# A third chunk without transposes: loading x transposed and normalising it in place, in an MLP beside a long convolution

## The chip, the cores and the metric

The kernel runs on one core of one Trainium2 chip. The metric is the device time of one execution in microseconds (us); the runs shown are the median of three. The engines are TensorE (PE, with PEld for its weight loads), VectorE (DVE), ScalarE (ACT), GpSimd (POOL) and SyncE (SP). Each works through its own queue strictly in the order written there. An instruction that waits holds up all behind it on its engine.

## The reference

```python
xn = _layernorm(x)                       # x = A_q, (1, 2048, 448)
# A: gated long convolution
k_shift = sum of 4 shifted k * shift_k   # causal, per channel
kv = k_shift * v
y  = irfft(rfft(kv, 4096) * rfft(ssm_k, 4096))[:2048] + kv * ssm_D
# B: MLP with the Mish activation
h  = xn @ w1 + b1                        # 448 -> 1792
b  = (h * tanh(softplus(h))) @ w2        # 1792 -> 448
return x + xn * y + b
```

All inputs and outputs are float32.

## The kernel before

**MLP.** The 2048 positions are cut into 8 chunks of 256 (two halves of 128), the hidden features into 7 pairs of 128-wide blocks. That gives 56 pairs of (chunk, block pair), worked through in order. Each pair has two slots (half steps): in the even one the first layer's 20 matmuls (`g1_mm`, line 510), in the odd one the activation (`mish`, line 518) and the second layer's 12 matmuls (`g2_mm`, lines 542 to 544) of the pair two before. Float32 accuracy comes from splitting each operand into a high part (a cast on ACT: ach, XH) and a low part (a subtraction on DVE: acl, XL) and multiplying three times. A chunk's second layer accumulates in two PSUM tiles, one for each half; DVE evacuates them into qt (`g2_evac`, L549, two instructions), and since there are only these two tiles, the next chunk's second layer may start only when the evacuation has freed them.

**The chunk's normalised, transposed x.** The first layer needs xn with features on the partitions. Chunks below `NT` (0 to 3) get it by transposes: bn_stats, bn_aggr and eps (L404, L407, L410: ve) on DVE, a power and the normalisation (L413, L417, L421) on POOL, eight PE transposes through PSUM (L462), and the split from PSUM (L474 on ACT, L472 on DVE). Chunks from `NT` on load x already transposed (`xT_load`, L432). Their mean and 1/std are computed on the same two DVE lines and by the power on POOL (mv<-ve), stored to DRAM by a DMA that POOL issues (`nt_store`, L440: MR), and loaded back by SP as a row broadcast to 128 partitions (`nt_row`, L443), one half at a time into one buffer (con). DVE then subtracts and multiplies in place (`nt_norm`, two L449 for each half), and the result is split (`nt_split`: L456 on ACT, L457 on DVE).

**Convolution.** Its first stage transforms eight groups of kv, KV0 to KV7, at the slots 24, 29, 34, 39, 44, 50, 55 and 59. Per group: four taps of the short convolution on DVE (L187, L190, L192 multiply, L197 adds, L200 multiplies with v), then 16 small matmuls (`f1_mm`, L144) into the PSUM tiles pq and pr, which ACT copies in part (L150) and DVE folds in two instructions (L154), and the result leaves by DMA. One multiplication of each group (the third tap) is done on POOL (`taps_pool`, L180): a one-element memset on DVE (L179), written just before the fold of the group ahead, lets it start, and the L197 behind the fold takes its result.

**What sets the order.** A plan by slots: `at` puts a step ahead of a slot's own work, `after` behind it. The tables at the head hold each step's place relative to the slot b where a chunk begins: q the query load, x the transposed load, stats, flush (what is left of the statistics is written out), row, norm and split for the two halves. The statistics' small instructions are handed out one by one between the taps (`dv`, the list `drip`). For chunk `NT` itself b is one slot later (line 665), and line 664 gives the tighter table `NT_ENDS` to the chunks 4 and 7. Line 674 and the lines above it write the plan down; `mlp_slot` (L557) holds the steps of the transposed chunks.

Of the kernel before, what the change touches and what calls it, by code (L numbers as in the profile page):

```python
# [19 lines left out]
NCHUNK = S // CH  # L20
# [9 lines left out]
I2_AT = {100: ((6, 7, 0, 1), 92, (95, 97, 98, 99), (0, 2, 0, 1)),  # L30
         108: ((2, 3, 4, 5), 101, (104, 105, 106, 107), (0, 1, 0, 1))}
LATE = 2
NT = 4
NT_AT = {"q": -5, "x": -1, "stats": -2, "flush": 0, "row": (4, 8), "norm": (7, 10), "split": (8, 11)}
NT_ENDS = dict(NT_AT, row=(4, 5), norm=(4, 7), split=(6, 8))
WARM_N = (448, 448, 448)
FILL_N = (224, 112, 96)

# [2 lines left out]
def tile_kernel(ctx: ExitStack, tc, q, qT, k, v, sk, hT, sD, w10, w1, w2, c_fib, c_g, c_gi, c_i2, out):  # L41
# [20 lines left out]
    E = dp.tile([NJ * 4, 64, D], F32, name="E")  # L62
    MR = {c: dp.tile([2, CH], F32, name="MR") for c in range(NT, NCHUNK)}

# [8 lines left out]
    def rs(c):  # L73
        return rstd[:, 2 * c:2 * c + 2] if c < NT else mv[:, 2 * c:2 * c + 2, 1]

# [26 lines left out]
    def dv(n=1):  # L102
        for _ in range(n):
            if drip:
                drip.pop(0)()
# [4 lines left out]
    def at(slot, fn, *args):  # L110
        plan.setdefault(int(slot), []).append((fn, args))

    def after(slot, fn, *args):
        plan2.setdefault(int(slot), []).append((fn, args))
# [278 lines left out]
    def xn_tile():  # L393
        return mp.tile([128, 4, CH], F32, name="xn", bufs=1)

    def ln_parts(c):
        st = mp.tile([128, 2, 6], F32, name="bst", bufs=2)
        ve = mp.tile([128, 2], F32, name="ve", bufs=2)
        if c < NT:
            XN[c] = xn = xn_tile().rearrange("p a b -> p (a b)").rearrange("p (j d) -> p j d", j=2)  # L400
        eng = nc.gpsimd if 0 < c < NCHUNK - 1 else V

        def stats(jj):
            V.bn_stats(st[:, jj], Q[c][:, jj])  # L404

        def aggr(jj):
            V.bn_aggr(mv[:, 2 * c + jj], st[:, jj])  # L407

        def eps(a, b):
            V.tensor_scalar(ve[:, a:b], mv[:, 2 * c + a:2 * c + b, 1], EPS, None, op0=ALU.add)  # L410

        def power(a, b):
            nc.gpsimd.tensor_tensor(rs(c)[:, a:b], ve[:, a:b], mhalf[:, a:b], op=ALU.pow)  # L413

        def norm(jj):
            j = 2 * c + jj
            eng.tensor_scalar(xn[:, jj, :D], Q[c][:, jj], mv[:, j, 0:1], rs(c)[:, jj:jj + 1],  # L417
                              op0=ALU.subtract, op1=ALU.mult)

        def tail(a, b, copy=eng.tensor_copy):  # L420
            copy(xn[:, a:b, D:], xn[:, a:b, D - 64:D])  # L421

        return stats, aggr, eps, power, norm, tail, ve
# [52 lines left out]
    def ln_T(c, jj):  # L476
        if jj == 0:
            dv(len(drip))
            x_tiles(c)
        p = pg()  # L480
        transposes(c, jj, p)
        for lo in range(2):
            x_split(c, jj, p, lo)
# [73 lines left out]
    def mlp_slot(s):  # L557
# [3 lines left out]
        if half == 0:  # L561
            if i < n:
                c, p = pairs[i]
                if c + 1 < NT:
                    if p == 0:
# [8 lines left out]
        else:  # L574
            if i < n:
                c, p = pairs[i]
                if p == NP - 2 and c + 1 < NT:
                    ln_T(c + 1, 0)
# [82 lines left out]
        GB[46 + i] = n  # L661

    for c in range(NT, NCHUNK):
        at_ = NT_ENDS if c in (NT, NCHUNK - 1) else NT_AT
        b = 2 * NP * (c - 1) + (1 if c == NT else 0)
        at(b + at_["q"], ln_load, c)
        at(b + at_["x"], xT_load, c)
        at(b + at_["stats"], nt_stats, c)
        at(b + at_["flush"], lambda: dv(len(drip)))
        for jj in range(2):  # L670
            at(b + at_["row"][jj], nt_row, c, jj)
            after(b + at_["norm"][jj], nt_norm, c, jj)
            after(b + at_["split"][jj], nt_split, c, jj)
# [28 lines left out]
    stats, aggr, eps, power, norm, tail, ve = ln_parts(0)  # L702
# [120 lines left out]
```

## Time and profile before

| | us |
|---|---|
| median of 3 runs | 359.58 (359.16 to 359.68) |
| the profiled execution | 359.25, of which its span is 357.5 |
| PE busy in the span | 351.8 (98%) |
| DVE busy | 269.7 (75%) |
| ACT busy | 157.0 (44%) |
| POOL busy | 76.1 (21%) |
| granted TensorE clock | 0.998 |

A row of a timeline gives the start (us from the span's start), the duration, engine, line, operation, out<-in, shape and count; in brackets stands the idle time ahead of it and what ended that. Matmuls overlap: the distance between their starts tells what they cost, not their duration. A row with count 2 is two instructions merged.

### The profile page before, as it was taken

The page shows a single profiled execution, that of the slowest core. Times are in us where ns is not written, and L with a number is a line of the kernel's source. Part 1 is how long each engine was busy: PE and PEld are TensorE (multiplying, and loading weights), DVE is VectorE, ACT ScalarE, POOL GpSimd, SP SyncE. Part 2 cuts the span into 40 slices and gives each one's busy share as a digit, 9 for nine tenths or more (in the row PEclk, how much of TensorE's full clock was granted, in tenths as well). Part 3 has the DMA queues.
Part 4 walks back from the last instruction along what each step waited for, and adds up shares of the span by engine and source line. Part 5 has one row for each costly group of instructions (what it writes and reads, how often), then busy time and mean ns, then how long its engine had stood idle before and what let it go on. Part 6 is the DMA issues. An engine that isn't in the chain of part 4 may idle for free.

```text
span 357.5 us, 7447 instructions
## 1 busy us (share of the span) xinstructions
PE 351.8 (98%) x3100; PEld 290.2 (81%) x3100; DVE 269.7 (75%) x371; ACT 157.0 (44%) x267; POOL 76.1 (21%) x81
## 2 busy tenths in 40 slices
PE   8999999999999999999999999999999999999995
PEld 2988888888888989888997758667775699979795
DVE  5989658999998899999537757756863933788942
ACT  4976552344232443343233453455445343354480
POOL 2037002821128240204000030011031116040030
PEclk9999999999999999999999999999999999999999
DMA  7998978749585536665969669999985386989076
GB/s 237 349 383 308 403 290 240 224 153 267 148 276 187 161 107 175 216 162 92 233 198 345 239 166 302 228 287 306 285 261 131 81 242 263 405 311 285 26 115 142
DMA packets 30227, 82.48 MB, mean 231 GB/s; under 512 B 3057, under 2 KB 15474, under 8 KB 30194
## 3 DMA queue, kind: packets, MB, share of 16 engines
q1 hardware_dynamic: 21410, 47.03, 38.7%
q0 software_dynamic: 4896, 22.95, 22.9%
q10 hardware_dynamic: 3888, 12.03, 12.6%
q8 instruction: 24, 0.39, 0.5%
q14 instruction: 9, 0.07, 0.1%
HBM read 53.55 MB, written 28.45 MB: 229 GB/s over the span
## 4 chain that ended last, share of the span: by engine, by line
PE 52%; DVE 5%; issue 1%
PE pq L510 7%; PE pg L542 7%; PE pg L544 7%; PE pg L543 6%; PE pp L510 5%; PE pr L510 4%; PE pp L233 3%; PE pr L233 3%; PE pp L272 2%; PE pg L510 2%; PE pq L233 2%; PE pr L272 1%; DVE x L197 1%; PE pp L326 1%; DVE acl L83 0%
## 5 line engine op out<-in xcount | busy, mean ns | idle before, releaser
L542 PE MATMUL pg<-w2h,ach 128*128 128x448 f32 x224 | 82.4, 368 | 0.0
L544 PE MATMUL pg<-w2h,acl 128*128 128x448 f32 x224 | 81.4, 363 | 0.0
L543 PE MATMUL pg<-w2l,ach 128*128 128x448 f32 x224 | 81.2, 363 | 0.0
L83 DVE TENSOR_TENSOR acl<-a,ach 128x512 fp32r<-128x512 f32 x56 | 38.8, 693 | 32.1 <-ACT ach L82 31.9
L518 ACT ACTIVATE a<-pg,b1t 128x256 f32<-128x256 f32 x66 | 27.9, 473 | 64.7 <-PE pg L510 57.9
L510 PE MATMUL pg<-XH,w1h 128*128 128x256 f32 x264 | 52.8, 283 | 0.1
L542 PEld LDWEIGHTS pg<-w2h,ach 128*128 128x128 f32 x224 | 41.9, 187 | 10.8 <-issue 6.5
L510 PEld LDWEIGHTS pg<-XH,w1h 128*128 128x128 f32 x264 | 41.3, 188 | 7.2 <-issue 5.6
L543 PEld LDWEIGHTS pg<-w2l,ach 128*128 128x128 f32 x224 | 42.1, 188 | 2.5
L544 PEld LDWEIGHTS pg<-w2h,acl 128*128 128x128 f32 x224 | 42.1, 188 | 2.4
L510 PE MATMUL pg<-XL,w1h 128*128 128x256 f32 x264 | 42.8, 277 | 0.0
L154 DVE TENSOR_TENSOR st<-pq,st 128x896 f32<-128x896 f32 x32 | 34.8, 1088 | 5.1 <-ACT st L150 4.5
L510 PEld LDWEIGHTS pg<-XL,w1h 128*128 128x128 f32 x264 | 35.9, 188 | 0.0
L82 ACT CAST ach<-a 128x512 fp32r<-128x512 f32 x56 | 34.8, 622 | 1.7
L180 POOL TENSOR_TENSOR x<-kr,skb 128x896 f32<-128x896 f32 x8 | 17.0, 2126 | 83.1 <-DVE x L179 70.5
L510 PE MATMUL pg<-XH,w1l 128*128 128x256 f32 x198 | 33.5, 278 | 0.0
L510 PEld LDWEIGHTS pg<-XH,w1l 128*128 128x128 f32 x198 | 27.6, 188 | 0.0
L197 DVE TENSOR_TENSOR x<-x 128x896 f32<-128x896 f32 x24 | 26.4, 1098 | 0.9 <-POOL x L180 0.3
L518 ACT ACTIVATE a<-pq,b1t 128x256 f32<-128x256 f32 x20 | 8.4, 472 | 31.8 <-PE pq L510 31.8
L283 POOL DMA_DIRECT2D E<-qe x14 | 8.7, 628 | 63.1 <-ACT qe L280 63.1
L150 ACT COPY st<-pr 128x896 f32<-128x896 f32 x16 | 14.5, 907 | 14.1 <-PE pr L144 12.1
L144 PE MATMUL pq<-x,con 32*64 32x448 f32 x128 | 15.9, 560 | 0.5 <-DVE x L200 0.5
(138 smaller groups left out, 601.3 us busy)
## 6 DMA issues: line engine op xcount, KB each, us to landing
Dkv<-st ACTq DMA_DIRECT2D x16, 448.0 KB, 6.3
ah<-Dh SPq DMA_DIRECT2D x8, 896.0 KB, 8.4
av<-Dkv SPq DMA_DIRECT2D x8, 896.0 KB, 8.8
e<-E POOLq DMA_DIRECT2D x8, 896.0 KB, 7.3
E<-qe POOLq DMA_DIRECT2D x14, 448.0 KB, 6.0
kr<-in_k_dram SPq DMA_DIRECT2D x10, 448.0 KB, 6.6
Dh<-st ACTq DMA_DIRECT2D x10, 448.0 KB, 6.4
x<-in_hT_dram SPq DMA_DIRECT2D x8, 448.0 KB, 6.6
```

Source lines behind the costliest of these rows:

```text
L82: nc.scalar.copy(h, raw)
L83: V.tensor_sub(l, raw, h)
L144: nc.tensor.matmul(ps[h][64 * jj:64 * jj + 64, b, :D], f1[rg:rg + 32], x[rg:rg + 32, jj], start=True, stop=True, tile_position=(rg, 64 * jj))
L154: f(st[:, n], e, st[:, 1])
L180: nc.gpsimd.tensor_mul(o, KR[g - u // 2], skb[:, u:u + 1].to_broadcast([128, 2, D]))
L197: V.tensor_add(KV[g], KV[g], o)
L233: nc.tensor.matmul(p[32 * t:32 * t + 32, r, :D], g[rs, t, c], a[rs, t], start=True, stop=True, tile_position=(64 * r, 32 * t))
L510: nc.tensor.matmul(ps[n], l, r, start=all(m[0] != n for m in seq[:n_]), stop=all(m[0] != n for m in seq[n_ + 1:]))
L518: nc.scalar.activation(a[:, n], ps[n], AF.Mish, bias=b1t[:, 2 * p + n:2 * p + n + 1])
L542: nc.tensor.matmul(ps, ah[:, n, cs], w2h[:, f], start=f == 0, stop=False)
L543: nc.tensor.matmul(ps, ah[:, n, cs], w2l[:, f], start=False, stop=False)
L544: nc.tensor.matmul(ps, al[:, n, cs], w2h[:, f], start=False, stop=f == NF - 1)
```

## The change

Chunk 3 joins the chunks that are loaded transposed (`NT` is 3). Its slot b is 29, and chunk 4's, which was 43, is now 42, since only the first such chunk gets the extra slot. The tight table now goes to the chunks 3, 4 and 7 under the name `NT_SOON`; its numbers are unchanged. Chunk 5 gets a table of its own: the query load three slots sooner, statistics and flush two slots sooner.

```diff
-NT = 4
+NT = 3
 NT_AT = {"q": -5, "x": -1, "stats": -2, "flush": 0, "row": (4, 8), "norm": (7, 10), "split": (8, 11)}
-NT_ENDS = dict(NT_AT, row=(4, 5), norm=(4, 7), split=(6, 8))
+NT_SOON = dict(NT_AT, row=(4, 5), norm=(4, 7), split=(6, 8))
+NT_HOW = {c: NT_SOON for c in (3, 4, 7)}
+NT_HOW[5] = dict(NT_AT, q=-8, stats=-4, flush=-2)
...
     for c in range(NT, NCHUNK):
-        at_ = NT_ENDS if c in (NT, NCHUNK - 1) else NT_AT
+        at_ = NT_HOW.get(c, NT_AT)
         b = 2 * NP * (c - 1) + (1 if c == NT else 0)
```

What that does to the queues is seen in the order of the instructions. Line numbers of the changed kernel are higher by 2. First POOL's whole stretch between chunk 2's normalisation and the convolution's second part, before:

```order
L180 TENSOR_TENSOR x<-kr,skb 128x896 x3
L413 TENSOR_TENSOR rstd<-ve,mhalf 128x2
L417 TENSOR_SCALAR xn<-qt,mv,rstd 128x448
L421 COPY xn<-xn 128x64
L417 TENSOR_SCALAR xn<-qt,mv,rstd 128x448
L421 COPY xn<-xn 128x64
L180 TENSOR_TENSOR x<-kr,skb 128x896
L413 TENSOR_TENSOR mv<-ve,mhalf 128x2
L440 DMA MR<-mv 128x2x2
L180 TENSOR_TENSOR x<-kr,skb 128x896 x3
L413 TENSOR_TENSOR mv<-ve,mhalf 128x2
L440 DMA MR<-mv 128x2x2
```

The same stretch of POOL after the change:

```order
L182 TENSOR_TENSOR x<-kr,skb 128x896
L415 TENSOR_TENSOR mv<-ve,mhalf 128x2
L442 DMA MR<-mv 128x2x2
L182 TENSOR_TENSOR x<-kr,skb 128x896 x3
L415 TENSOR_TENSOR mv<-ve,mhalf 128x2
L442 DMA MR<-mv 128x2x2
L182 TENSOR_TENSOR x<-kr,skb 128x896 x2
L415 TENSOR_TENSOR mv<-ve,mhalf 128x2
L442 DMA MR<-mv 128x2x2
L182 TENSOR_TENSOR x<-kr,skb 128x896
```

Chunk 3's power moved from behind KV3's tap (the third of the first row) to ahead of KV2's, now with a store instead of two normalisations; chunk 5's power moved ahead of KV7's tap, which was the last of three. On DVE, from the acl ahead of KV2's taps to the L197 behind the next fold (KV1's), before:

```order
L83 TENSOR_TENSOR acl<-a,ach 128x512
L187 TENSOR_TENSOR x<-kr,skb 128x896
L190 TENSOR_TENSOR x<-kr,skb 128x448
L192 TENSOR_TENSOR x<-kr,skb 128x448
L197 TENSOR_TENSOR x<-x 128x896
L83 TENSOR_TENSOR acl<-a,ach 128x512
L179 MEMSET x 1x1
L154 TENSOR_TENSOR st<-pq,st 128x896 x2
L197 TENSOR_TENSOR x<-x 128x896
```

The same stretch of DVE after the change:

```order
L406 BN_STATS bst<-qt 128x6
L189 TENSOR_TENSOR x<-kr,skb 128x896
L406 BN_STATS bst<-qt 128x6
L192 TENSOR_TENSOR x<-kr,skb 128x448
L409 BN_AGGR mv<-bst 128x2
L194 TENSOR_TENSOR x<-kr,skb 128x448
L409 BN_AGGR mv<-bst 128x2
L199 TENSOR_TENSOR x<-x 128x896
L412 TENSOR_SCALAR ve<-mv 128x2
L85 TENSOR_TENSOR acl<-a,ach 128x512
L181 MEMSET x 1x1
L156 TENSOR_TENSOR st<-pq,st 128x896 x2
```

Chunk 3's five statistics moved in between KV2's taps, ahead of the memset; they stood in the fold of KV2 and behind it. On PE two rows of four transposes, ahead of and behind the second layer's matmuls of slot 39, are gone, and nothing else moves. The rest of DVE's and SP's order follows the tables: four L449 and two L457 of chunk 3 among the taps of KV3 and KV4, and chunk 3's transposed load and two row loads on SP.

## The prediction

> **What bounds the kernel now.** I read the page's first two parts (PE busy in every slice, clock full), then the busy time by stretches, then the timelines of TensorE (PE), VectorE (DVE) and GpSimd (POOL).
>
> ```profile
> 94.00:126.00 32.00, 32.00 (x253) 28.37 (x252) 30.00 (x43) 11.31 (x21) 12.24 (x7) 1.00 0.70 209
> ```
>
> The columns are the stretch, its length, then the busy time of PE, PEld, DVE, ACT and POOL. Around the edit PE never rests and DVE works 30.00 of 32 us. PE sets the end; DVE hardly keeps up with it as long as the key-value groups (KV0 to KV7) run. Wherever DVE falls behind, PE waits. It does once:
>
> ```profile
> 156.80 0.62 PE L510 MATMUL pg<-XL,w1h 128*128 128x256 f32 x4
> 157.34 0.59 PE L144 MATMUL pq<-x,con 32*64 32x448 f32 x2
> 167.86 0.62 PE L510 MATMUL pg<-XL,w1h 128*128 128x256 f32 x4
> 169.01 0.59 PE L144 MATMUL pq<-x,con 32*64 32x448 f32 x2 [0.53 <-DVE x L200]
> 161.27 0.06 DVE L179 MEMSET x<- 1x1 f32 x1
> 162.26 1.38 DVE L410 TENSOR_SCALAR ve<-mv 128x2 f32<-128x2 f32 x1
> 164.55 1.08 DVE L197 TENSOR_TENSOR x<-x 128x896 f32<-128x896 f32 x1
> 167.86 1.09 DVE L200 TENSOR_TENSOR x<-x 128x896 f32<-128x896 f32 x1
> 161.49 2.12 POOL L180 TENSOR_TENSOR x<-kr,skb 128x896 f32<-128x896 f32 x1 [12.62 <-issue]
> ```
>
> From the last matmuls of a pair to the next group's first one PE takes 157.34 - 156.80 = 0.54; at KV7 it takes 1.15, since L200 ends at 168.95. The stall is 0.61. Its root stands above: chunk 5's two-column ve ran 1.38 and ended at 163.64, just when POOL's tap ended (163.61).
>
> **Transposes gone: -0.76.** The only work that leaves PE is chunk 3's eight transposes. The stretch that holds them is set against the same stretch of slots 55 and 56, without transposes:
>
> ```profile
> 113.26 0.62 PE L510 MATMUL pg<-XL,w1h 128*128 128x256 f32 x4
> 120.14 0.62 PE L510 MATMUL pg<-XL,w1h 128*128 128x256 f32 x4
> 162.92 0.63 PE L510 MATMUL pg<-XL,w1h 128*128 128x256 f32 x4
> ```
>
> 120.14 - 113.26 = 6.88 against 162.92 - 156.80 = 6.12: 0.76, all on the path. POOL's two normalisations go too; POOL is not on the path.
>
> **Chunk 3's statistics, from slot 34 to 27.** The order shows two bn_stats, two bn_aggr and ve spread over KV2's taps; on POOL the power and the MR store now stand ahead of KV2's tap.
>
> ```profile
> L404 DVE BATCH_NORM_STATS2 bst<-qt 128x6 f32<-128x448 f32 x16 | 9.6, 618 | 2.7 <-DMA qt<-in_q_dram 2.7
> L407 DVE BATCH_NORM_AGGREGATE mv<-bst 128x2 f32<-128x6 f32 x16 | 2.6, 173 | 0.1
> L410 DVE TENSOR_SCALAR ve<-mv x9: 153/169/1376, 4.5 to 260.5; 128x2 f32<-128x2 f32 x7, 128x1 f32<-128x1 f32 x2
> 87.47 0.68 DVE L83 TENSOR_TENSOR acl<-a,ach 128x512 fp32r<-128x512 f32 x1
> 90.48 1.09 DVE L197 TENSOR_TENSOR x<-x 128x896 f32<-128x896 f32 x1
> 95.41 1.15 DVE L549 TENSOR_TENSOR qt<-pg,qt 128x448 f32<-128x448 f32 x2
> 96.47 2.21 DVE L154 TENSOR_TENSOR st<-pq,st 128x896 f32<-128x896 f32 x2
> 128.41 0.69 DVE L83 TENSOR_TENSOR acl<-a,ach 128x512 fp32r<-128x512 f32 x1
> 128.57 1.09 POOL L413 TENSOR_TENSOR mv<-ve,mhalf 128x2 f32<-128x2 f32 x1 [8.21 <-DVE ve L410]
> 129.96 0.83 POOL L440 DMA_DIRECT2D MR<-mv  x1 [0.30 <-POOL mv L413]
> 131.39 2.12 POOL L180 TENSOR_TENSOR x<-kr,skb 128x896 f32<-128x896 f32 x1 [0.60 <-DVE x L179]
> 163.72 0.72 POOL L413 TENSOR_TENSOR mv<-ve,mhalf 128x2 f32<-128x2 f32 x1
> L413 POOL TENSOR_TENSOR rstd<-ve,mhalf x5: 552/730/1555, 4.7 to 107.4; 128x2 f32<-128x2 f32 x3, 128x1 f32<-128x1 f32 x2
> 97.84 0.36 PE L542 MATMUL pg<-w2h,ach 128*128 128x448 f32 x1
> 100.34 0.59 PE L144 MATMUL pq<-x,con 32*64 32x448 f32 x2
> ```
>
> DVE's share: 2 x 0.62 + 2 x 0.17 + 0.17 = 1.75, less 0.08 each, since the next instruction starts that much before an end (the two L549 take 1.15 and L154 starts 1.06 after them): 1.35. So ve, now just ahead of the acl at 87.47, ends at about 88.90. Behind it on POOL come the power, a gap of 0.30, the store's 0.83 and only then the tap's 2.12. The power has two prices in these rows, 1.09 and 0.72, and took 1.55 at the most (the last L413 row, at 107.4). In the row with 1.09 an acl was running, and in the new order an acl follows ve at once, so I take 1.09, with 0.72 and 1.55 as ends. The tap then ends at 88.95 + 1.09 + 0.30 + 0.83 + 2.12, about 93.32, and L197, which adds it, runs at 93.36, not 90.48: DVE is 2.88 late, of which the wait for POOL is 1.53.
>
> The Trainium skill, page "SBUF — State Buffer", section "Who interferes with whom", says that a DVE instruction with two SBUF inputs keeps out a GpSimd instruction that reads SBUF until it ends, whichever issued first holding the port. By that rule the power would end some 0.56 behind the acl, and the two rows agree (0.72 beside a fold that reads PSUM); without it the median of 0.73 would do, and the sum below would be 0.36 lower.
>
> Who waits: chunk 2's first second-layer matmul (97.84) needs the accumulator that the first L549 frees. That ends at 95.41 + 0.62 + 2.88 = 98.91, PE starts 0.06 later: a stall of 1.13. KV2's matmuls (100.34) need the fold that ended at 98.68, now 101.56: 0.14 more than the 1.13. PE is 1.27 late, and 0.51 once the transposes are gone.
>
> **Normalisation and split of chunk 3, chunk 4's steps a slot sooner.**
>
> ```profile
> 109.57 1.49 DVE L200 TENSOR_TENSOR x<-x 128x896 f32<-128x896 f32 x1
> 113.82 1.33 DVE L197 TENSOR_TENSOR x<-x 128x896 f32<-128x896 f32 x1
> 116.06 0.69 DVE L472 TENSOR_TENSOR XL<-pg,XH 128x512 fp32r<-128x512 f32 x1 [0.92 <-ACT XH L474]
> 117.45 0.69 DVE L83 TENSOR_TENSOR acl<-a,ach 128x512 fp32r<-128x512 f32 x1 [0.70 <-ACT ach L82]
> 124.32 1.09 DVE L200 TENSOR_TENSOR x<-x 128x896 f32<-128x896 f32 x1
> 134.99 1.14 DVE L549 TENSOR_TENSOR qt<-pg,qt 128x448 f32<-128x448 f32 x2
> 139.97 1.41 DVE L449 TENSOR_TENSOR xn<-xn,con 128x512 f32<-128x512 f32 x2
> 143.10 0.69 DVE L83 TENSOR_TENSOR acl<-a,ach 128x512 fp32r<-128x512 f32 x1 [0.72 <-ACT ach L82]
> 128.00 0.59 PE L144 MATMUL pq<-x,con 32*64 32x448 f32 x2
> 136.47 0.36 PE L542 MATMUL pg<-w2h,ach 128*128 128x448 f32 x1
> ```
>
> Until KV4's L200, DVE gains two pairs of L449 (2 x 1.33 start to start) and part of chunk 4's statistics (two bn_stats, one bn_aggr: 1.17). It loses chunk 3's statistics at their old place (1.35), its idle gaps at the transposes (0.92 + 0.70) and what two instructions took above 1.09 while POOL normalised (0.40 + 0.24). The low halves L457 and L472 cost the same. Lateness: 2.88 + 2.66 + 1.17 - 1.35 - 1.62 - 0.64 = 3.10. L200 ends at 125.41 + 3.10 = 128.51, and PE wants it at 128.00 + 0.51 = 128.51: no stall, but no margin.
>
> Chunk 2's evacuation is next. Chunk 4's statistics no longer lie in between: lateness 3.10 - 1.17 = 1.93. Its first L549 ends at 137.53; PE, due at 136.98, starts at 137.59: 0.61. PE's lateness is 1.12.
>
> What moves on SP's queue is the transposed load, the two row loads and the query load of chunk 3, and the steps of chunks 4 and 5. The second row load waits for the first half's normalisation, since both halves use one row buffer, and behind it stand the key load of KV4 and chunk 4's query load; at chunk 4 the first row comes ahead of KV6's key load, and the second ahead of chunk 2's result, chunk 5's query load (which reuses the result's buffer and waits for it to leave) and KV6's value load. I price all of it at nothing: DVE, 2 to 3 us late, comes to each load's first use later than before, and a key that is late by less than that keeps nobody. Without this cover it is the second rival. On ACT the two casts XH<-xn take the place of two casts from PSUM; ACT has room (11.31 of 32 us).
>
> **Chunk 5's statistics, two half steps sooner.** ve now precedes the memset that starts the tap, so it should take 0.17. The tap then bounds the fold: L197 runs at 161.27 + 0.15 + 2.12 + 0.04 = 163.58 relative to the old times, 0.97 sooner than 164.55. With the gap of 0.72 absorbed DVE is 1.93 - 0.72 - 0.97 = 0.24 late at KV7: L200 ends at 169.19. PE, without the old stall, wants it at 168.40 + 1.12 = 169.52. The stall of 0.61 is gone. If ve still met a tap, 0.97 would come back, less the margin of 0.33.
>
> **Sum.** -0.76 + 1.13 + 0.14 + 0.61 - 0.61 = +0.51. The profiled execution took 359.25 (span 357.5 and 1.75 around it), 0.33 below the median of 359.58. So 359.76 in its terms and 360.1 on the median. With the power at 0.72 or 1.55 it is +0.14 or +0.97: 359.7 to 360.6.
>
> **Rivals.** The first: the tap isn't held up, because POOL runs it beside the store or DVE has more room than I found. For it: no row shows a tap directly behind a store. Against: POOL's rows never overlap, and its order is fixed. Then DVE is only 1.35 late: L549 ends at 97.38, before 97.84, and the fold at 100.03, before 100.34. PE is 0.76 early; KV4 holds (126.98 against 127.24); chunk 2's evacuation is 0.39 late and PE loses some 0.35. With the old stall gone that is -0.76 + 0.35 - 0.61 = -1.02: 358.6, faster.
>
> The second: the row of chunk 4 comes late.
>
> ```profile
> DMA to landing us min/median/max: 3.2/5.2/8.6
> DMA to landing us min/median/max: 3.6/4.7/9.2
> ```
>
> The first row is the MR store's, the second the row load's. Chunk 4's store leaves at about 130.6 and DVE reaches the first L449 at 139.97 - 0.60 + 1.93 = 141.30 (the acl that stood before it now follows). The medians make 140.5, in time. If the two together take over 10.7, DVE waits, and the key load behind the row on SP's queue comes late as well; at 8.6 + 4.7 it is 2.6, of which 0.33 is covered: +0.51 + 2.27, 362.4, slower. For it: in chunk 5 the store took the 8.6. Against: at chunk 4's place it has landed near the minimum before. The Trainium skill, page "DMA: Bandwidth & Descriptors", section "Anatomy of one DMA — SWDGE (gpsimd) path", gives 2.0 us and a size term for a GpSimd DMA; this 2 KB store would by that estimate land in 2.0, and the rival could not occur. The rows say 3.2 at least, so they decide, and it stays open.
>
> **How the numbers follow.** The forecast gets 0.55, the first rival 0.25, the second 0.20. Within 0.2% is 358.86 to 360.30, about what a measurement of this kernel can tell from no change. Of the forecast's 0.55 some 0.12 lies above (power beyond 1.3, or KV4 without margin). Faster 0.25, same 0.43, slower 0.32. The range runs from just under the first rival, 358.3, to 361.6, inside the second; the forecast's own is 359.7 to 360.6.
>
> **What would show it.** On POOL the power, the store and a tap in a row near 89 to 93, and L197 waiting 1.5 for POOL; PE waiting for L549 at 98 and at 137; no wait for L200 at KV7 and ve at 0.17; the stretch around 113 to 120 shorter by 0.76. I am wrong if L197 doesn't wait, if PE waits for L200 at KV4, or if L449 waits for its row.

## The result and the profile after

| | us |
|---|---|
| before, median of 11 runs | 359.41 (359.05 to 359.89) |
| after, median of 11 runs | 360.19 (359.95 to 360.86) |
| ratio after to before | 1.0021, 95% interval 1.0011 to 1.0031 |
| span of the profiled execution, before and after | 357.5 and 358.8 |

The change makes the kernel 0.78 us slower. That is 0.21%, with an interval from 0.11 to 0.31%, so it is slower than before, and just about at the 0.2% that the prediction took as the least it could tell from no change. The forecast was 360.1, with 358.3 to 361.6 as its range. Of all the executions behind this document one was disturbed, 899.18 us of the kernel with three more transfers, and its ratio is taken without it.

The first fence shows timeline rows of the changed kernel around KV2's taps: DVE, then POOL, then PE. Its line numbers are higher by 2 (L199 is the old L197, L551 the old L549, L412 ve, L415 the power, L442 the MR store, L182 POOL's tap).

```profile
89.08 0.16 DVE L412 TENSOR_SCALAR ve<-mv 128x2 f32<-128x2 f32 x1
89.15 0.69 DVE L85 TENSOR_TENSOR acl<-a,ach 128x512 fp32r<-128x512 f32 x1
93.73 1.09 DVE L199 TENSOR_TENSOR x<-x 128x896 f32<-128x896 f32 x1 [1.76 <-POOL x L182]
98.67 1.15 DVE L551 TENSOR_TENSOR qt<-pg,qt 128x448 f32<-128x448 f32 x2
89.32 1.08 POOL L415 TENSOR_TENSOR mv<-ve,mhalf 128x2 f32<-128x2 f32 x1 [13.45 <-DVE ve L412]
90.70 0.83 POOL L442 DMA_DIRECT2D MR<-mv  x1 [0.29 <-POOL mv L415]
91.56 2.14 POOL L182 TENSOR_TENSOR x<-kr,skb 128x896 f32<-128x896 f32 x1
97.95 0.62 PE L512 MATMUL pg<-XL,w1h 128*128 128x256 f32 x4
99.34 0.47 PE L544 MATMUL pg<-w2h,ach 128*128 128x448 f32 x1 [0.77 <-DVE qt L551]
99.65 0.36 PE L545 MATMUL pg<-w2l,ach 128*128 128x448 f32 x1
101.99 0.59 PE L146 MATMUL pq<-x,con 32*64 32x448 f32 x2
```

Power, store and tap stand in a row on POOL. The tap ends at 93.70, which is 4.46 behind ve; the working had 4.42. L199 waits 1.76 for it. PE then waits for L551: from the last first-layer matmuls to the second layer it takes 99.34 - 97.95 = 1.39, and where nothing is late 0.45 (97.60 - 97.15 in the fence of the first experiment), so the stall is 0.94. From there to KV2's matmuls it takes 2.65 against 2.50 before: 0.15 more. Of that, 0.11 lies in the first step behind the stall, which takes 0.31 (99.34 to 99.65) where before it took 0.20 (97.84 to 98.04).

The next rows of the changed kernel belong to the missing transposes, KV4, chunk 2's evacuation and KV7.

```profile
114.91 0.62 PE L512 MATMUL pg<-XL,w1h 128*128 128x256 f32 x4
121.03 0.63 PE L512 MATMUL pg<-XL,w1h 128*128 128x256 f32 x4
127.86 1.09 DVE L202 TENSOR_TENSOR x<-x 128x896 f32<-128x896 f32 x1
129.01 0.59 PE L146 MATMUL pq<-x,con 32*64 32x448 f32 x2
137.02 0.62 PE L512 MATMUL pg<-XL,w1h 128*128 128x256 f32 x4
137.94 0.44 PE L544 MATMUL pg<-w2h,ach 128*128 128x448 f32 x1 [0.31 <-DVE qt L551]
160.18 0.17 DVE L412 TENSOR_SCALAR ve<-mv 128x2 f32<-128x2 f32 x1
169.42 0.62 PE L512 MATMUL pg<-XL,w1h 128*128 128x256 f32 x4
169.96 0.59 PE L146 MATMUL pq<-x,con 32*64 32x448 f32 x2
```

The stretch that held the transposes takes 6.12 in place of 6.88: 0.76 gained. At KV4 the matmuls start at 129.01, 0.06 behind the end of L202 (128.95); from PE's last matmul before them it takes 0.38 (128.63 to 129.01) in place of 0.30 (127.70 to 128.00), so PE waits 0.08 there. Chunk 2's L551 costs 0.92 - 0.45 = 0.47. Chunk 5's ve takes 0.17, and KV7's matmuls follow after 0.54: the old stall of 0.61 is gone.

So far the terms, without KV4's, make -0.76 + 0.94 + 0.15 + 0.47 - 0.61 = +0.19. Most of the rest is at the end of the program. The fence has, of the changed kernel and then of the kernel before, the last evacuations on DVE and the group of SP's semaphore waits once the last result has landed (the columns of the group: times of one in ns, first and last start).

```profile
353.72 0.62 DVE L551 TENSOR_TENSOR qt<-pg,qt 128x448 f32<-128x448 f32 x1 [3.51 <-PE pg L546]
L820 SPq EVENT_SEMAPHORE  x8: 28/28/28, 357.5 to 357.9; - x8
352.67 0.62 DVE L549 TENSOR_TENSOR qt<-pg,qt 128x448 f32<-128x448 f32 x1 [3.51 <-PE pg L544]
L818 SPq EVENT_SEMAPHORE  x3: 28/28/28, 356.5 to 356.6; - x3
```

From the first of the last two evacuations to the end it is 358.8 - 353.7 = 5.1 after and 357.5 - 352.7 = 4.8 before. SP works off eight waits instead of three, 0.06 apart: 5 x 0.06 = 0.30. No term of the forecast had that. With it the sum is +0.5. About 0.25 more lies in three steps of 0.08: KV4's wait, the first second-layer matmul behind chunk 2's stall, which takes 0.28 to the next (137.94 to 138.22) instead of 0.20, and a slightly slower first layer near 174. Together these make about 0.75, near the 0.78 measured. One further difference of the two profiled executions isn't the change's: PE comes 0.56 later to KV0's matmuls near 48, ahead of everything that was edited. In the other profiles that same place lies between 0.3 earlier and 1.2 us later than in the profile of before.

### The profile page after: what moved, and what is told of

Same layout as the page of the kernel before. It is cut to its first block, busy times and chain, and to the rows that moved or that the text cites. A ratio compares the mean times of both kernels' runs of the same rounds, so it can differ in the third digit from the quotient of the medians.

```text
span 358.8 us, 7434 instructions
## 1 busy us (share of the span) xinstructions
PE 352.3 (98%) x3092; PEld 289.8 (81%) x3092; DVE 270.2 (75%) x375; ACT 156.6 (44%) x267; POOL 73.5 (20%) x78
## 4 chain that ended last, share of the span: by engine, by line
PE 60%; issue 4%; DVE 3%; POOL 1%
PE pg L544 8%; PE pg L546 8%; PE pg L545 8%; PE pq L512 7%; PE pg L512 6%; PE pp L512 5%; PE pr L512 4%; PE pr L235 3%; PE pp L235 3%; PE pp L274 2%; PE pq L235 2%; PE pr L274 1%; PE pp L328 1%; DVE x L199 1%; PE pq L146 1%
## 5 line engine op out<-in xcount | busy, mean ns | idle before, releaser
L182 POOL TENSOR_TENSOR x<-kr,skb 128x896 f32<-128x896 f32 x8 | 17.0, 2130 | 68.1 <-DVE x L181 42.1
L199 DVE TENSOR_TENSOR x<-x 128x896 f32<-128x896 f32 x24 | 26.2, 1090 | 3.0 <-POOL x L182 2.3
L415 POOL TENSOR_TENSOR mv<-ve,mhalf 128x2 f32<-128x2 f32 x5 | 5.4, 1084 | 73.1 <-DVE ve L412 73.1
```

The lines of the kernel that those rows point to most:

```text
L182: nc.gpsimd.tensor_mul(o, KR[g - u // 2], skb[:, u:u + 1].to_broadcast([128, 2, D]))
L199: V.tensor_add(KV[g], KV[g], o)
```

## The experiments

**The tap first.** The working held the order on POOL responsible. This kernel changes only that.

```diff
+        held = [lambda: (power(0, 2), nt_store(c))]
+        if c == 3:
+            HELD.extend(held)
         drip.extend([lambda: stats(0), lambda: stats(1), lambda: aggr(0), lambda: aggr(1),
-                     lambda: (eps(0, 2), power(0, 2), nt_store(c))])
+                     lambda: (eps(0, 2), *[f() for f in held if c != 3])])
...
             after(t, taps_pool, g + 1, 2)
+        if g == 1:
+            after(t, lambda: HELD.pop()())
```

> The changed kernel with one thing in another order: on POOL chunk 3's power and MR store stand behind KV2's tap, not ahead of it; DVE, PE, ACT and SP keep their order. My theory (the tap is held up by power and store): L199 behind KV1's fold no longer waits 1.76 for POOL, DVE is 1.76 sooner, chunk 1's L551 and the fold come in time, and chunk 2's L551 too, so the three stalls of 0.94, 0.15 and 0.47 go: 360.2 - 1.56 = 358.6, faster than before by 0.2%. Rival (DVE's longer list alone makes it late; POOL's order is no matter): 360.2 as the change. Second rival (chunk 3's row is now late, since the store leaves some 2.3 later; in the changed kernel it landed 5.0 ahead of its use): the three stalls go, but L451 waits for its row; it has about 1.0 to spare, and each us above that comes back at a later stall.

Measured: 358.68, against 359.27 before on the same chip, ratio 0.9976 (0.9968 to 0.9985). Rows of POOL, DVE and PE:

```profile
89.18 2.13 POOL L182 TENSOR_TENSOR x<-kr,skb 128x896 f32<-128x896 f32 x1 [14.12 <-PE pg L549]
91.25 0.72 POOL L415 TENSOR_TENSOR mv<-ve,mhalf 128x2 f32<-128x2 f32 x1
92.27 0.83 POOL L445 DMA_DIRECT2D MR<-mv  x1 [0.29 <-POOL mv L415]
91.34 1.09 DVE L199 TENSOR_TENSOR x<-x 128x896 f32<-128x896 f32 x1 [0.18 <-POOL x L182]
97.15 0.62 PE L515 MATMUL pg<-XL,w1h 128*128 128x256 f32 x4
97.60 0.36 PE L547 MATMUL pg<-w2h,ach 128*128 128x448 f32 x1
```

With the same work in the same order on DVE, L199 waits 0.18 instead of 1.76, and PE goes on after 0.45. At chunk 2's L551 PE takes 0.52 (135.05 to 135.57), so of the stall of 0.47 only 0.07 is left. The two ratios, 1.0021 and 0.9976, lie 0.0045 or 1.6 us apart, as the three stalls (0.94 + 0.15 + 0.47 = 1.56) would have it. The change is slower because of the order of three POOL instructions. DVE's longer list alone doesn't make it so, and no wait for chunk 3's row took the place of the stalls.

**Chunk 3's statistics one half step sooner still.** The same end by the table, one line added.

```diff
+NT_HOW[3] = dict(NT_SOON, q=-6, stats=-3, flush=-1)
```

> The changed kernel with chunk 3's statistics and query load one half step sooner (stats -3, flush -1, q -6): ve lies before KV2's long taps, so power and store are over when the memset lets the tap start, while DVE does the same work. My theory: the same as with the tap first, 358.6, and the row comes sooner rather than later. Rival (DVE's longer list alone makes it late): 360.2. Second rival (the power, now beside other DVE instructions, or the statistics ahead of KV1's second fold hold up the fold and with it PE at KV2 or ACT): between 358.6 and 359.6.

Measured: 358.60, ratio 0.9980 (0.9971 to 0.9988), the same as with the tap first.

```profile
86.65 1.02 POOL L416 TENSOR_TENSOR mv<-ve,mhalf 128x2 f32<-128x2 f32 x1 [11.34 <-DVE ve L413]
87.97 0.83 POOL L443 DMA_DIRECT2D MR<-mv  x1 [0.30 <-POOL mv L416]
89.53 2.12 POOL L183 TENSOR_TENSOR x<-kr,skb 128x896 f32<-128x896 f32 x1 [0.73 <-DVE x L182]
91.69 1.09 DVE L200 TENSOR_TENSOR x<-x 128x896 f32<-128x896 f32 x1 [0.19 <-POOL x L183]
```

The store is through 0.73 before the memset lets the tap start. The half step in the change's table was the one that put power and store exactly into the tap's time.

**Chunk 5's table, taken away and alone.**

```diff
-NT_HOW[5] = dict(NT_AT, q=-8, stats=-4, flush=-2)
```

> The changed kernel without chunk 5's own table (its statistics at the old place). My theory: ve meets KV7's tap again, takes about 1.4 instead of 0.17, DVE is 0.97 later at KV7's L202, of which 0.10 is covered, so PE stalls 0.6 to 0.9 there: 360.8 to 361.1. Rival (the old stall at KV7 would be covered by PE's lateness of 1.12, so the part on chunk 5 brings nothing here): 360.2.

Measured: 360.38, ratio 1.0027 (1.0017 to 1.0036). The converse is the kernel before with that table and nothing else:

> The kernel before with nothing but chunk 5's earlier query load, statistics and flush. My theory: the stall of 0.61 at KV7 goes and nothing takes its place: before - 0.61, 358.8 on 359.4. Rival (a later wait of DVE or of a transfer takes its place): no change, 359.4.

Measured: 358.77, ratio 0.9987 (0.9977 to 0.9996), 0.50 under the 359.27 of the same chip. Alone the table is worth, within its interval, the 0.61 that the forecast gave it. In the changed kernel its absence costs some 0.2 by the two ratios (1.0027 against 1.0021), where 0.6 to 0.9 was expected. Their intervals leave about 0.5 either way, so the time alone decides neither for the theory nor for the rival; the stall does. Rows of the kernel without it:

```profile
162.84 1.38 DVE L411 TENSOR_SCALAR ve<-mv 128x2 f32<-128x2 f32 x1
168.44 1.09 DVE L201 TENSOR_TENSOR x<-x 128x896 f32<-128x896 f32 x1
168.59 0.62 PE L511 MATMUL pg<-XL,w1h 128*128 128x256 f32 x4
169.59 0.59 PE L145 MATMUL pq<-x,con 32*64 32x448 f32 x2 [0.39 <-DVE x L201]
```

ve meets the tap again and takes 1.38. But DVE is only 168.44 - 167.86 = 0.58 later than before there, where the working would give 1.93 - 0.72 = 1.21, and PE itself comes 168.59 - 167.86 = 0.73 later. So the stall is 1.00 - 0.54 = 0.46, and part of the old 0.61 is covered by PE's own lateness. The rival had the direction, but PE's lateness covers only 0.15 of the stall, not all of it.

**The end of the program.** In one kernel chunk 6's result leaves in one transfer, so that SP issues one fewer; in the other the kernel before gets three more.

```diff
-            if late(c):
+            if c == NCHUNK - 1:
                 nc.sync.dma_start(out[:, 2 * c + jj], x[:, jj])
+            elif late(c) and jj:
+                nc.sync.dma_start(out[:, 2 * c:2 * c + 2], x)
```

> The kernel c3_m3 with chunk 6's result stored by one transfer in place of two, so SP issues one transfer fewer. In all runs with chunk 3 transposed the program's end, from the last L551's start on, is 0.30 longer (5.11 against 4.81): after the last result has landed SP works off 8 waits of 0.06 each, where the kernel before has 3. Theory: SP ends on a wait for each of 8 semaphores in a fixed order, the transfers take them in turn, and three more transfers moved the last one from the sixth to the first. With one transfer fewer it has the eighth: 1 wait in place of 8, 7 x 0.06 = 0.43 less, 358.6 - 0.43 = 358.2, and 4.68 from the last L551. Rival (the longer end comes from the transfers in flight or from chance): 358.6, and 5.11.

```diff
-        nc.sync.dma_start(out[:, 2 * c:2 * c + 2], Q[c])
+        if c < 3:
+            for jj in range(2):
+                nc.sync.dma_start(out[:, 2 * c + jj], Q[c][:, jj])
+        else:
+            nc.sync.dma_start(out[:, 2 * c:2 * c + 2], Q[c])
```

> The kernel before with the results of chunks 0, 1 and 2 stored by two transfers each in place of one: three more transfers on SP, all else as it was. Theory of the semaphores' turn: the last transfer takes the first of the eight, SP has 8 waits behind it in place of 3, the end is 5.11 in place of 4.81, and the time is before + 0.3: 359.6 on 359.3. Rival: no change, 359.3, and 4.81.

The group of SP's waits behind the last landing, first with one transfer fewer, then with three more:

```profile
L823 SPq EVENT_SEMAPHORE  x1: 28/28/28, 355.7 to 355.7; - x1
L822 SPq EVENT_SEMAPHORE  x8: 28/28/28, 356.9 to 357.4; - x8
```

One wait and eight, as the turn of the semaphores has it. The times go the same way, though these runs alone would not carry it: 358.42 with ratio 0.9971 (0.9960 to 0.9981) against 0.9980 of the same kernel without the edit, and 359.90 against 359.46, ratio 1.0007 (0.9996 to 1.0019). The profile of the kernel with three more bears it out: from 48 on, PE stays 0.45 to 0.47 behind the kernel before up to its last matmuls, and from the last two evacuations to the end it takes 5.1 instead of 4.8. The edit with one transfer fewer, made on the kernel with the tap first:

> The kernel tapfirst with chunk 6's result stored by one transfer in place of two. Theory of the semaphores' turn: 358.7 - 0.43 = 358.2 to 358.3. Rival: 358.7.

Measured: 358.12, ratio 0.9962 (0.9950 to 0.9974). It is faster than both kernels.

**A late row, made to happen.** The second rival was chunk 4's row coming late. Here, in the kernel c3_m3, chunk 4's power and store are held behind KV5's tap, by the edit of the first experiment with other numbers.

```diff
+        if c == 4:
+            HELD.extend(held)
...
+        if g == 4:
+            after(t, lambda: HELD.pop()())
```

> The kernel c3_m3 with chunk 4's power and MR store held behind KV5's tap on POOL, the other queues unchanged. It makes happen what the second rival of the prediction feared: the store leaves 5.2 later, the row load, which landed 1.9 ahead of its first use, lands about 3.3 behind it. Theory: L452 waits about 3.3 for the row, DVE hands it on to PE at KV6 less 0.3: 358.6 + 3.0, so 361.1 to 361.9. Rival (DVE has idle time enough behind it, or the row lands sooner): 358.6 to 359.5.

Measured: 365.41, ratio 1.0162 (1.0149 to 1.0176): 6.8 above c3_m3, where 2.5 to 3.3 was expected. Three rows of the timeline, then the busy time by stretches (the columns are those of the prediction's first fence, PE's clock third from the right):

```profile
145.10 1.42 DVE L455 TENSOR_TENSOR xn<-xn,con 128x512 f32<-128x512 f32 x2 [5.55 <-DMA con<-MR]
156.47 0.62 PE L516 MATMUL pg<-XL,w1h 128*128 128x256 f32 x4
160.81 1.01 PE L147 MATMUL pq<-x,con 32*64 32x448 f32 x2 [3.72 <-DVE x L203]
```

```profile
157.00:160.00 3.00, 0.08 (x1) 0.00 (x0) 2.93 (x5) 2.13 (x5) 0.00 (x0) 0.88 0.98 271
160.00:164.00 4.00, 3.19 (x20) 1.67 (x21) 3.97 (x9) 0.91 (x1) 0.08 (x1) 0.50 0.45 153
164.00:168.00 4.00, 4.00 (x22) 3.70 (x21) 3.93 (x7) 0.00 (x0) 2.99 (x3) 0.74 0.02 1
168.00:172.00 4.00, 4.00 (x28) 3.84 (x27) 3.85 (x5) 1.47 (x3) 0.85 (x1) 1.00 0.13 27
```

DVE waits 5.55 for the row, of which PE feels 3.8 (160.81 - 156.47, less the usual 0.54). The granted clock falls to 0.50 meanwhile, and KV6's first matmuls take 1.01 instead of 0.59; the span is 6.2 longer than c3_m3's (363.1 against 356.9), 2.4 more than the stall. The stretches show when: a mean of 0.88 over 157 to 160 puts the fall near 159.3, which is 2.2 behind the end of PE's last matmuls (157.09), and 0.74 over 164 to 168 puts the return to full clock near 166.1, which is 5.3 after PE went on. The Trainium skill, page "TensorE: Matmul & The Clock Gate", section "What's actually happening", says that the array falls to half its clock after an idle window of about 3.4 us and comes back after as long a busy one. The trace shows the half clock, but other lengths: it fell after 2.2 of idle and came back after 5.3 of work.

**Smaller stalls at the same place.** Two instructions more on DVE ahead of KV6's L202.

```diff
+        if (g, u) == (6, 3):
+            for _ in range(2):
+                V.tensor_tensor(KV[g], KV[g], KV[g], op=ALU.max)
         if u == 3:
```

> The kernel c3_m3 with two more instructions on DVE ahead of KV6's L202 (each the maximum of the tile with itself, 1.12 from start to start), so that PE stalls there for about 2.0 in place of the 3.7 of row4_late. In row4_late the granted clock fell to 0.50 and 0.74 in the two stretches behind that stall, and 2.4 were lost beyond it. Theory (a stall costs its own length; the clock falls only behind one as long as 3.7): clock 1.0 throughout, 358.6 + 1.9 = 360.5. Rival (any stall of some us lowers the clock): 361.5 or more, with a granted clock under 0.9 behind it.

Measured: 361.07, ratio 1.0037 (1.0025 to 1.0049); against c3_m3's ratio of 0.9980 that is 0.0057, some 2.0 us.

```profile
157.44 0.59 PE L147 MATMUL pq<-x,con 32*64 32x448 f32 x2 [0.57 <-DVE x L206]
169.99 0.59 PE L147 MATMUL pq<-x,con 32*64 32x448 f32 x2 [1.52 <-DVE x L206]
168.00:172.00 4.00, 2.48 (x26) 1.52 (x25) 3.11 (x4) 2.35 (x4) 0.00 (x0) 1.00 0.99 259
```

The lateness comes to PE in two pieces, 0.57 at KV6 and 1.52 at KV7, and the clock stays at 1.00. Stalls of up to 1.5 cost their own length and 3.8 costs more; where between the two it changes wasn't tried, since no stall of 2 came about. The fall after 2.2 of idle says only that it can be well below 3.8.

**Chunk 4 at its old slots.** The changed kernel with one undone.

```diff
-        b = 2 * NP * (c - 1) + (1 if c == NT else 0)
+        b = 2 * NP * (c - 1) + (1 if c in (3, 4) else 0)
```

> The changed kernel with chunk 4's steps back at their old slots, one later. The prediction priced this part at nothing. Theory: its statistics (1.17 on DVE) then lie behind KV4's L202 instead of ahead of it, where PE waited only 0.08; the work up to chunk 2's L551 is the same, so the stall of 0.47 there stays: 360.0 to 360.3. Rival (sooner was what made DVE late at chunk 2's L551): the stall of 0.47 goes, 359.7. Second rival (the row or the low half of chunk 4 now comes late for PE): 360.6 or more.

Measured: 360.68, ratio 1.0028 (1.0017 to 1.0038), which cannot be told from the change's 1.0021. The first two rows are the changed kernel's, the next four this one's:

```profile
120.60 0.68 DVE L85 TENSOR_TENSOR acl<-a,ach 128x512 fp32r<-128x512 f32 x1
137.18 1.14 DVE L551 TENSOR_TENSOR qt<-pg,qt 128x448 f32<-128x448 f32 x2
120.23 0.69 DVE L85 TENSOR_TENSOR acl<-a,ach 128x512 fp32r<-128x512 f32 x1
137.25 1.14 DVE L551 TENSOR_TENSOR qt<-pg,qt 128x448 f32<-128x448 f32 x2
136.58 0.62 PE L512 MATMUL pg<-XL,w1h 128*128 128x256 f32 x4
138.01 0.44 PE L544 MATMUL pg<-w2h,ach 128*128 128x448 f32 x1 [0.81 <-DVE qt L551]
```

The stall at chunk 2's L551 stays, and is 138.01 - 136.58 - 0.45 = 0.98 in place of 0.47. In this execution PE and DVE both came about 0.4 earlier to this stretch (136.58 against 137.02, 120.23 against 120.60), but DVE lost that again: between its two rows it has the same instructions, and needs 17.02 in place of 16.58. So moving chunk 4 a slot sooner wasn't what made DVE late there; in these two profiles it made the stall smaller. The time is in the second rival's range (360.6 or more), but its reason isn't seen: PE waits for no row and no low half of chunk 4.

**The evacuation one instruction sooner.** On the kernel with the tap first and one transfer fewer, chunk 2's two L551 go ahead of the add that stood before them.

```diff
-        if s % 2 == 0 and j >= 0 and pairs[j][1] == NP - 1:
+        if s % 2 == 0 and j >= 0 and pairs[j][1] == NP - 1 and pairs[j][0] != 2:
             g2_evac(pairs[j][0])
...
         mlp_slot(s)
+        if s == 2 * (3 * NP + G2_LAG) - 1:
+            g2_evac(2)
```

> The kernel tapfirst_one with chunk 2's two L551 written ahead of the add L199 that stood before them on DVE; nothing else moves. In that kernel's profile PE still loses 0.23 and 0.08 at this place, and the accumulator was complete before DVE came to it. Theory: L551 starts 1.0 sooner, both go: 358.1 - 0.3 = 357.8. Rival (the accumulator is not complete so soon, DVE waits for it and is late at KV5's L202): 358.1 or more.

PE's rows, of tapfirst_one and then of this kernel:

```profile
135.57 0.62 PE L515 MATMUL pg<-XL,w1h 128*128 128x256 f32 x4
136.25 0.44 PE L547 MATMUL pg<-w2h,ach 128*128 128x448 f32 x1
136.49 0.62 PE L515 MATMUL pg<-XL,w1h 128*128 128x256 f32 x4
136.94 0.36 PE L547 MATMUL pg<-w2h,ach 128*128 128x448 f32 x1
```

The distance falls from 0.68 to 0.45: the stall is gone. (In the second execution PE comes 0.92 later to this place and DVE 0.81, so some 0.1 of the 0.23 isn't the edit's.) The time, 358.10 (357.69 to 359.12), ratio 0.9958 (0.9944 to 0.9972), can't be told from the 0.9962 without it. So the place is settled and the gain in time isn't.

## Why the prediction came out

- **Transposes gone: -0.76.** Measured 0.76 on the stretch.
- **Tap held up behind power and store.** The mechanism and its place are shown by the tap put first, which removes the stall and all but 0.07 of the one that follows from it at chunk 2. The power took 1.08 where I chose 1.09. DVE came 98.67 - 95.41 = 3.26 late to L551, of which 0.49 was there before the change's first step (84.16 against 83.67 at the acl ahead of it): 2.77, where the working had 2.88. PE was itself 0.56 later by then, 0.07 more than DVE. So the stall was 0.94 and not 1.13. The 0.14 set for KV2's fold came as 0.15, by luck: 0.11 of it is the slower first step behind the stall, which the working didn't have, and only the rest can be the fold's.
- **The rule on the shared port.** At 89.32 the power ended 0.56 behind the acl (89.84 to 90.40), as the Trainium skill, page "SBUF — State Buffer", section "Who interferes with whom", would have it. Behind the tap, in the first experiment, it took 0.72.
- **KV4 without margin.** PE did wait for L202 there, by 0.08, which the prediction had named as a sign of being wrong. The working set L200's end and the time at which PE wants it equal at 128.51, and left out the 0.06 between such an end and PE's start that its own rows show at KV7 (168.95 to 169.01). Chunk 4's row was in time.
- **Chunk 2's evacuation: +0.61.** Measured 0.47.
- **Chunk 5: -0.61.** The stall is gone and ve takes 0.17. As the worth of that part of the change it was too much: alone it gives 0.50, and in the changed kernel it saves a stall of 0.46 in place of 0.61, since PE, late itself, would have covered part of it.
- **Row loads at nothing.** Held: no L451 of chunks 3 and 4 waited. But that rival's price was wrong both ways. When the row was made late, DVE's lateness was covered by 1.8 at KV6 (5.55 to 3.8), where the working let 0.33 pass as cover, and beyond that the clock took 2.4.
- **The first rival, 358.6.** The tap put first is that case, and it came out at 358.68. In terms of before on the same chip it was -0.59 and not -1.02: 0.30 of the difference is SP's end, the rest small steps.

So the total agrees for a partly lucky reason. The forecast difference was +0.51 and the measured one +0.78; the times, 360.1 and 360.19, lie closer than that because the median of before came out at 359.41, not 359.58. Within the sum, the stalls were 0.32 too large (1.88 against 1.56), and the 0.30 of SP's end and the 0.25 of small steps were missing. The failed step is "What moves on SP's queue ... I price all of it at nothing": three more transfers cost nothing where they are issued, and 0.30 at the end.

## What to carry to other kernels

When a step moves sooner, look on each engine's queue for what it now stands ahead of: a power and a store of 2.2 us together, on an engine off the critical path, turned a gain of 0.6 into a loss of 0.8. Moving them one more half step ahead, or behind the tap, undid it. And price two parts of a change both alone and together: a stall removed late in the program is worth less once another part has made the waiting engine late anyway.

## What was not expected of the hardware

- In this program SP ends on a row of waits 0.06 apart, and how many of them come behind the last landing depends on how many transfers were issued before: eight, three or one, up to 0.43 us.
- In a PE stall of 3.8 us the granted clock fell to 0.50 some 2.2 us after the last matmul and was full again only 5.3 us after PE went on; that cost 2.4 us beyond the stall. Stalls up to 1.5 us left the clock at 1.00.
- The same DVE instructions took 16.58 or 17.02 us by their order alone. In the rows of the timeline an instruction that uses the result of the one before starts 0.03 behind its end, another one 0.08 ahead of it; small independent instructions between dependent ones fill these gaps. That this makes all of the 0.44 is argued, not shown.
